# One product of a scaled V moved from VectorE to GpSimd in a fused attention and maxout kernel

## The chip, the cores and the metric

The kernel runs on one core of one Trainium2 chip. The metric is the device time of one execution in microseconds. A core has five engines that run their own instruction queues in order and meet at semaphores: TensorE (PE in the profile, with its weight loads as PEld), VectorE (DVE), ScalarE (ACT), GpSimd (POOL) and SyncE (SP), which here only issues DMAs.

## The reference

Four batches of eight heads over 768 positions of 64 dims are attended, causally in all heads, and in "streaming" heads only to 4 sink positions and a window of 64. Its output, laid out as 3072 tokens by 512, goes through a maxout layer with three weights of 512 x 768 and an output weight of 768 x 512.

```python
scores = scale * np.matmul(q, k.transpose(0, 1, 3, 2))
...
stream_keep = causal & (is_sink | in_win)
...
a = np.exp(scores)
a = a / (np.sum(a, axis=-1, keepdims=True) + 1e-09)
return np.matmul(a, v).astype(np.float32)
...
h = np.maximum(np.maximum(x @ w1, x @ w2), x @ w3)
return (h @ w_out).astype(np.float32)
```

## The kernel before, in words

The attention is cut into 16 steps. Step t belongs to batch t // 4, to half (t // 2) % 2 of the query positions, and to four heads (t % 2), which form two pairs i = 0 and 1. A batch's halves have 384 positions each, three blocks of 128. So step 2 is batch 0, second half, heads 0 to 3; step 3 the same with heads 4 to 7; step 4 begins batch 1.

A step goes through these functions:

- `scores(t, u)`: for each unit u of a step (two in a first half, four in a second) TensorE forms transposed scores in PSUM (L441) out of the tile KQ, ScalarE takes their exponentials into the fp16 tile pt (L452), and `masks` multiplies parts of pt by the head's mask in place (L479). This product is done by GpSimd, but for eight triples of step, pair and unit in the list `MASK_ON_DVE`, which VectorE does; (3, 0, 0), (3, 0, 1) and (3, 1, 3) are among them. The PSUM tiles of the scores come from a pool of two buffers.
- `prep_v(t, i, op, vf_engine)`: makes the fp16 values of a pair. First `op` casts the loaded fp32 values vs into va (L392). Then `vf_engine` multiplies them by the flags `far` of the heads into vf (L394), which is used for key blocks two or more behind the query block. In a second half vf is made from va for three blocks, 128 x 384 elements; so it waits for the cast.
- `av(t, i)`: TensorE multiplies pt by va and vf into one PSUM bank (L495; 30 matmuls in a second half), and VectorE takes the reciprocals of the sums (L503) and scales into x (L505).
- x is turned into xT either by a DMA transpose on SP's queue (L514, all steps in `BY_DMA`, step 2 among them) or by TensorE and a copy (`turn_x`; step 3).
- `ffn(b, half)`: a generator that yields after each group of matmuls. A group of four matmuls makes 128 x 384 of one of the three products (L338). The first weight's result is copied to acc by ScalarE (L346), the second and third are joined with it by VectorE's maximum (L349, into acc, and then hT). For batch 0 all groups of the first weight come first, then the second, then the third: six groups each. After them each of three blocks is multiplied by the output weight woutt (L364), copied to ot by ScalarE (L370) and written out by SP's queue (L371). The queue `fill(n)` emits n pieces of this work at a time.

The PSUM banks of `av`, of the transposes and of `ffn` come in turn from one pool of four, so a group of matmuls may have to wait until the result of four groups before has been read.

For batch 0, k and q are cast and transposed on TensorE (`cast_pair`, `turn_pair`). For later batches `load` brings k and q in by GpSimd's DMA queue (L174) and `turn` transposes them in blocks on VectorE into KQ (L190), two instructions for k and two for q of each four heads. The values of batches 1 to 3 are loaded on SP's queue by `load_v`; those of the second half of batch 0 by GpSimd's queue.

The order of all this is written by hand. Steps 0 and 1 stand in straight code; from step 2 on the table `PROGRAM` has one row for each unit of scores. A row has a number of `ffn` pieces that are due, a flag on whether the two pairs' scores are apart, and four strings of other work: ahead of the scores, behind them, and after each part of the filling. In the strings, `v 2 0 ad` is `prep_v` for step 2 and pair 0, with its cast on ScalarE (a) and its product on VectorE (d); `ap` puts the product on GpSimd. `cast`, `pair`, `load`, `load_v`, `turn`, `av` and `x` are the functions above; `gate` makes SP's queue wait for an exponential of step 3 before it loads the next values.

The rows around the change, with the units that they belong to, are those of units 2 and 3 of step 2 and units 0 to 2 of step 3:

```python
(2.0, False, "", "pair 1 2", "load 1 1", ""),
(2.2, False, "pair 1 3", "v 2 0 ad", "", "v 2 1 ap"),
(2.2, False, "", "gate, load_v 1 0", "", ""),
(1.6, True, "", "av 2 0", "", "turn 1 0 0 0"),
(1.0, True, "turn 1 0 0 1", "", "av 2 1, turn 1 0 1 0", ""),
```

In the second of them VectorE copies a transposed pair (L162), scores of unit 3 are formed, pair 0's values are prepared, some pieces of `ffn` are emitted, and pair 1's values are prepared. Each engine's queue takes its own instructions in this order: VectorE has that copy, the product of pair 0, and then the maxima of the `ffn` pieces; GpSimd has two masks of unit 3 and then the product of pair 1.

Of the kernel before, what the change touches and what calls it, by code (L numbers as in the profile page):

```python
# [51 lines left out]
def kernel(  # L52
# [94 lines left out]
    def turn_pair(half, hp, *engines):  # L147
        if (0, hp // 2) not in KQs:
            KQs[0, hp // 2] = qkt.tile([P, 2, S, 2], FP16, tag="KQ", name="KQ")
        xs = cast.pop((half, hp))  # L150
        n = 2 // len(engines)
        for part, op in enumerate(engines):
            tr = bank([P, 1024], FP16, "tr")
            for i in range(n):
                for j in range(HB):
                    c = i * HALF + j * P
                    nc.tensor.transpose(
                        tr[:, c : c + P],
                        xs[part + i][:, j].rearrange("p h d -> p (h d)"),
                        ident,  # L160
                    )
            op(  # L162
                out=of_pair(hp)[
                    :, part : part + n, half * HALF : (half + 1) * HALF
                ].rearrange("p i (t j) -> p i t j", j=HB),
                in_=tr[:, 0 : n * HALF].rearrange("p (i j t) -> p i t j", i=n, j=HB),
            )
# [218 lines left out]
    def prep_v(t, i, op, vf_engine):  # L386
        b, half, qd = where(t)
        vs = staged_v[b, half]
        j, k0 = b % 2, half * HB
        hs = slice(4 * qd + 2 * i, 4 * qd + 2 * i + 2)  # L390
        vdst = va[j][:, hs, k0 : k0 + HB, 0:D]
        op(out=vdst, in_=vs[:, hs])  # L392
        k0, k1 = ((0, 1), (1, 4))[half]
        vf_engine.tensor_tensor(  # L394
            out=vf[j][:, hs, k0:k1, 0:D],
            in0=vs[:, hs, 0:1] if half == 0 else va[j][:, hs, k0:k1, 0:D],
            in1=far[:, hs, k0:k1].unsqueeze(3).to_broadcast([P, 2, k1 - k0, D]),
            op=ALU.mult,
        )
# [120 lines left out]
    def turn_x(t, i, op=None):  # L520
# [82 lines left out]
        (2.4, True, "", "", "cast 1 2 dp", ""),  # L603
        (2.4, False, "load 1 0", "", "cast 1 3 da", ""),
        (2.0, False, "", "pair 1 2", "load 1 1", ""),
        (2.2, False, "pair 1 3", "v 2 0 ad", "", "v 2 1 ap"),
        (2.2, False, "", "gate, load_v 1 0", "", ""),
        (1.6, True, "", "av 2 0", "", "turn 1 0 0 0"),
        (1.0, True, "turn 1 0 0 1", "", "av 2 1, turn 1 0 1 0", ""),
# [44 lines left out]
        v=lambda t, i, e: prep_v(int(t), int(i), ops[e[0]], engines[e[1]]),  # L654
# [6 lines left out]
        pair=lambda h, hp: turn_pair(int(h), int(hp), dve),  # L661
# [65 lines left out]
```

## Time and profile before

| what | us |
|---|---|
| median of four runs | 202.26 |
| lowest and highest of them | 201.56, 202.72 |
| the profiled execution, its own time | 202.22 |
| its span, first to last instruction | 200.3 |

| engine | busy us | share of the span |
|---|---|---|
| TensorE, matmuls | 189.4 | 95% |
| TensorE, weight loads | 109.3 | 55% |
| ScalarE | 131.6 | 66% |
| VectorE | 123.4 | 62% |
| GpSimd | 122.5 | 61% |

The granted TensorE clock is full speed (1.000) through the whole span. Of the 32 products into vf, 29 are on GpSimd and three on VectorE: two of 128 x 128 in the first half of batch 0 and the one of step 2's pair 0.

A row of the profile names the engine, the line of the kernel, the operation, the tile written and the tiles read (out<-in), the shape and type, and the count. In the timeline it is headed by the start in microseconds from the span's start and the length, and ends in brackets with how long the engine was idle before it and what ended that idle time. In the view of waits a row has who waited, for whom, the total in microseconds, how often, and the longest.

### The profile page before, as it was taken

What the parts mean: (1) busy time and instruction counts of PE and PEld (TensorE: products, weight loads), DVE (VectorE), ACT (ScalarE), POOL (GpSimd) and SP (SyncE); (2) the same over time, 40 slices, a digit from 0 to 9 for tenths busy, and PEclk for the clock granted to TensorE, in tenths of its full rate; (3) what the DMA queues carried; (4) which work ended last, traced back from release to release, by engine and by line L of the source; (5) the groups of instructions that cost most, each with busy time, mean ns of one, the idle gap of its engine ahead of it and who ended that gap; (6) DMA issues with size and microseconds to landing.
All of it is one profiled execution on the core that took longest, in us unless ns stands there. A gap on an engine that the chain in (4) does not pass through costs nothing.

```text
span 200.3 us, 5133 instructions
## 1 busy us (share of the span) xinstructions
PE 189.4 (95%) x2059; PEld 109.3 (55%) x2059; DVE 123.4 (62%) x242; ACT 131.6 (66%) x206; POOL 122.5 (61%) x153
## 2 busy tenths in 40 slices
PE   7897999796999999999999999999999999999992
PEld 2455554455566466574655465575555565755552
DVE  2798687999777838871554739961555234443540
ACT  4586798597875777666787685757768769313221
POOL 3599169579897915787969726699937547500000
PEclk9999999999999999999999999999999999999999
DMA  5999999997739993804359994502401250023004
GB/s 181 271 233 224 277 240 212 213 200 179 184 47 163 171 241 111 163 17 128 111 86 141 162 263 124 101 20 79 140 20 23 105 75 20 3 56 142 3 0 157
DMA packets 43245, 26.48 MB, mean 132 GB/s; under 512 B 33558, under 2 KB 38230, under 8 KB 43222
## 3 DMA queue, kind: packets, MB, share of 16 engines
q1 hardware_dynamic: 37206, 15.01, 35.0%
q0 software_dynamic: 4784, 10.23, 26.3%
q10 hardware_dynamic: 1232, 0.92, 1.5%
q8 instruction: 16, 0.26, 0.5%
q14 instruction: 7, 0.06, 0.1%
HBM read 25.17 MB, written 6.29 MB: 157 GB/s over the span
## 4 chain that ended last, share of the span: by engine, by line
PE 74%; DMA 10%; POOL 5%; DVE 3%; issue 2%; ACT 2%; SPq 1%; DVEq 0%; ACTq 0%; POOLq 0%
PE yy L338 39%; PE yy L364 13%; PE st L441 9%; PE oacc L495 9%; DMA vs<-in_v_dram 7%; PE yst L338 3%; DMA ks<-in_k_dram 2%; DVE KQ L190 2%; ACT pt L452 1%; DMA out_dram<-ot 1%; POOL vs L208 1%; POOL qs L126 1%; POOL ks L126 1%; PE yst L364 1%; ACT ot L370 1%
## 5 line engine op out<-in xcount | busy, mean ns | idle before, releaser
L479 POOL TENSOR_TENSOR pt<-pt,mk 128x512 f16<-128x512 f16 (+1 forms) x76 | 80.5, 1083 | 36.8 <-ACT pt L452 36.8
L452 ACT ACTIVATE pt<-st 128x1024 f16<-128x1024 f32 (+3 forms) x99 | 83.1, 894 | 21.1 <-PE st L441 20.3
L349 DVE TENSOR_TENSOR acc<-yy,acc 128x384 f16<-128x384 f32 x45 | 25.1, 558 | 28.3 <-PE yy L338 18.6
L338 PE MATMUL yy<-xT,w2t 128*128 128x384 f16 x180 | 35.9, 327 | 1.7 <-DVE hT L349 1.7
L338 PE MATMUL yy<-xT,w1t 128*128 128x384 f16 x180 | 36.1, 327 | 0.1
L338 PE MATMUL yy<-xT,w0t 128*128 128x384 f16 x180 | 35.6, 326 | 0.4 <-DVE xT L531 0.4
L346 ACT CAST acc<-yy 128x384 f16<-128x384 f32 x45 | 21.0, 485 | 17.0 <-PE yy L338 10.6
L364 PE MATMUL yy<-woutt,hT 128*128 128x512 f16 (+1 forms) x138 | 32.0, 375 | 0.0
L441 PE MATMUL st<-KQ 32*128 32x384 f16 (+4 forms) x560 | 28.5, 279 | 0.6 <-DVE KQ L190 0.5
L349 DVE TENSOR_TENSOR hT<-yy,acc 128x384 f16<-128x384 f32 x45 | 24.9, 558 | 6.7 <-PE yy L338 4.3
L495 PEld LDWEIGHTS <-pt 128*128 128x128 f16 x672 | 23.9, 97 | 5.4 <-issue 2.2
L338 PEld LDWEIGHTS <-w2t 128*128 128x128 f16 x192 | 17.6, 98 | 15.1 <-issue 4.0
L190 DVE STREAM_TRANSPOSE KQ<-kq 128x384 f32<-128x384 f32 x24 | 25.7, 1129 | 0.0
L338 PEld LDWEIGHTS <-w0t 128*128 128x128 f16 x192 | 18.2, 98 | 12.9 <-issue 1.0
L495 PE MATMUL oacc<-va,pt 128*128 128x65 f16 x352 | 24.8, 193 | 0.3 <-ACT va L392 0.3
L338 PEld LDWEIGHTS <-w1t 128*128 128x128 f16 x192 | 17.2, 98 | 12.8 <-issue 1.3
L370 ACT COPY ot<-yy 128x512 f32<-128x512 f32 x22 | 12.9, 588 | 15.5 <-PE yy L364 9.2
L495 PE MATMUL oacc<-vf,pt 128*128 128x65 f16 x320 | 21.1, 193 | 0.9 <-POOL vf L394 0.9
L364 PEld LDWEIGHTS <-hT 128*128 128x128 f16 x150 | 13.9, 98 | 14.5 <-issue 0.3
L441 PEld LDWEIGHTS <-KQ 32*128 32x128 f16 (+1 forms) x560 | 12.1, 93 | 17.3 <-issue 11.8
L505 DVE TENSOR_TENSOR x<-oacc,rc 128x384 f16<-128x384 f32 x32 | 17.8, 557 | 1.3 <-DVE rc L503 0.2
L503 DVE RECIPROCAL rc<-oacc 128x6 f32<-128x6 f32 x32 | 6.1, 192 | 20.1 <-PE oacc L495 20.0
(71 smaller groups left out, 130.0 us busy)
## 6 DMA issues: line engine op xcount, KB each, us to landing
out_dram<-ot SPq DMA_DIRECT2D x23, 256.0 KB, 3.1
vs<-in_v_dram SPq DMA_DIRECT2D x21, 256.0 KB, 6.1
kq<-in_k_dram POOLq DMA_DIRECT2D x6, 384.0 KB, 5.5
kq<-in_q_dram POOLq DMA_DIRECT2D x6, 384.0 KB, 7.7
qs<-in_q_dram ACTq DMA_DIRECT2D x4, 192.0 KB, 4.1
ks<-in_k_dram SPq DMA_DIRECT2D x4, 192.0 KB, 3.7
w0t<-in_moe_w_dram POOLq DMA_DIRECT2D x1, 768.0 KB, 7.2
ks<-in_k_dram POOLq DMA_DIRECT2D x2, 384.0 KB, 6.9
```

Of the source, the lines that this page charges most:

```text
L190: nc.vector.transpose(out=dst.rearrange("c (p j) -> c j p", j=n)[:, j0:j1], in_=src.rearrange("c (j i) -> c j i", i=R),)
L338: nc.tensor.matmul(yy[:, 0:HALF], w_t[wi][:, ks, ni * P : (ni + 1) * P], xT[b, half][ks].rearrange("p a t -> p (a t)"), start=(ks == 0), s ...
L346: nc.scalar.copy(out=acc[ni], in_=yy[:, 0:HALF])
L349: nc.vector.tensor_tensor(out=dst, in0=yy[:, 0:HALF], in1=acc[ni], op=ALU.max)
L364: nc.tensor.matmul(yo[:, 0:n], hT[ns][:, tb * P : (tb + 1) * P], woutt[:, ns, c : c + n], start=(ns == 0), stop=(ns == NNB - 1),)
L370: op(out=ot[:, c : c + n], in_=yo[:, 0:n])
L441: nc.tensor.matmul(sts[g // m][:, g % m, c0 : c0 + n * P], KQ[rows, 0, ki * P : (ki + 1) * P], KQ[rows, 1, t0 : t0 + n * P], start=(c0 == ...
L452: nc.scalar.activation(out=pts[t, i][:, u, h0 : h0 + m, 0:w], in_=st[:, :, 0:w], func=AF.Exp, scale=sc,)
L479: engine.tensor_tensor(out=x, in0=x, in1=m, op=ALU.mult)
L495: nc.tensor.matmul(o[:, qi, hl, 0 : D + 1], pt[:, u, hl, c : c + P], vv[:, 2 * hp + hl, ki, 0 : D + 1], start=(idx == 0), stop=(idx == len ...
L503: nc.vector.reciprocal(out=rc, in_=o[:, :, :, D])
L505: nc.vector.tensor_tensor(out=x, in0=o[:, :, :, 0:D], in1=rc.unsqueeze(3).to_broadcast([P, HB, 2, D]), op=ALU.mult,)
```

## The change

One letter of the table: the product that makes vf for pair 0 of step 2 is issued on GpSimd in place of VectorE. The cast into va stays on ScalarE, and the place in the program's order stays as it is, so that GpSimd's queue has two masks, the product of pair 0 and the product of pair 1.

```diff
-        (2.2, False, "pair 1 3", "v 2 0 ad", "", "v 2 1 ap"),
+        (2.2, False, "pair 1 3", "v 2 0 ap", "", "v 2 1 ap"),
```

## The prediction

> **What bounds the kernel now.** I read the page first, then the waits of TensorE (PE) over the whole span, and then the timeline of each engine around the moved instruction. The page's rows of busy time and of slices:
>
> ```profile
> PE 189.4 (95%) x2059; PEld 109.3 (55%) x2059; DVE 123.4 (62%) x242; ACT 131.6 (66%) x206; POOL 122.5 (61%) x153
> PE   7897999796999999999999999999999999999992
> ```
>
> TensorE is busy for 95% of the span, so the kernel is bound by TensorE nearly everywhere: a microsecond counts only if it shortens TensorE's own row. The waits of TensorE from 50 us to the end are one line, and over 30 to 50 us they are four (the last two lines below are of the same stretch, for ScalarE and GpSimd):
>
> ```profile
> PE st L441 <- DVE KQ L190: 0.5, 1, 0.5
> ...
> PE yy L338 <- DVE hT L349: 1.7, 1, 1.7
> PE oacc L495 <- POOL vf L394: 0.9, 1, 0.9
> PE tr L527 <- DVE x L505: 0.7, 1, 0.7
> ...
> ACT pt L452 <- PE st L441: 4.1, 4, 1.8
> POOL pt L479 <- ACT pt L452: 4.0, 3, 2.4
> ```
>
> The reader is to see two things. TensorE's longest wait here is 1.7 us, for VectorE's hT; and after 51 us it waits for almost nothing, so whatever TensorE is early at 51 us it is early at the end. The timelines of VectorE (DVE), GpSimd (POOL), ScalarE and TensorE show where the 1.7 us comes from (start, length, engine, line, count, idle time before it and what ended it):
>
> ```profile
> 30.98 0.95 DVE L162 COPY KQ<-tr 128x768 f16<-128x768 f16 x1
> 33.03 2.67 DVE L394 TENSOR_TENSOR vf<-va,far 128x384 f16<-128x384 f16 x1 [1.10 <-ACT va L392]
> 35.63 1.47 DVE L349 TENSOR_TENSOR hT<-yy,acc 128x384 f16<-128x384 f32 x3
> ...
> 33.00 2.27 POOL L479 TENSOR_TENSOR pt<-pt,mk 128x512 f16<-128x512 f16 x2
> 35.23 1.16 POOL L394 TENSOR_TENSOR vf<-va,far 128x384 f16<-128x384 f16 x1
> 36.35 0.66 POOL L479 TENSOR_TENSOR pt<-pt,mk 128x256 f16<-128x256 f16 x1
> 39.42 0.67 POOL L479 TENSOR_TENSOR pt<-pt,mk 128x256 f16<-128x256 f16 x1 [2.41 <-ACT pt L452]
> ...
> 33.74 0.82 PE L338 MATMUL yy<-xT,w2t 128*128 128x384 f16 x4
> 36.23 0.81 PE L338 MATMUL yy<-xT,w2t 128*128 128x384 f16 x4 [1.66 <-DVE hT L349]
> 36.97 0.61 PE L441 MATMUL st<-KQ 64*128 64x384 f16 x8
> ...
> 37.40 1.02 ACT L452 ACTIVATE pt<-st 128x1024 f16<-128x1024 f32 x1 [1.83 <-PE st L441]
> ```
>
> The DVE row at 33.03 is the instruction that the change moves. VectorE idles 1.10 us until ScalarE has cast va, and then sits in this product until 35.70, while GpSimd runs two masks that end at 35.27. Behind it in VectorE's queue stand three hT maxima; the first is done at 36.17, its PSUM bank comes free, and only then does TensorE start its sixth group of w2 (36.23), 1.66 us after the last matmul it had issued (33.74 to 34.56).
>
> **The change, part by part.**
>
> *Removed from VectorE:* one instruction of 2.67 us and the 1.10 us of idling for va ahead of it: 3.77 us in which VectorE did nothing else. The hT maxima behind it can start when their groups are ready. Groups 2 to 4 of w2 run on TensorE from 31.14 to 33.26, 0.65 us each, so their maxima (0.54 us each, from the row of three) end at about 32.5, 33.2 and 33.8. The bank for group 6 is free at 32.5, and TensorE goes on at 34.4 (the pitch after 33.74 is 0.65) instead of 36.23.
>
> *Added to GpSimd:* one product 128x384 f16. The fifteen such products that GpSimd already makes (vf from va, line 394) take 822 to 1158 ns, with a median of 829, so 0.83 us; the 1158 is the one at 35.23, which met VectorE's product at its end. It stands where the second pair's product stands now: GpSimd reaches it at 35.23, va having been cast by 33.4, so it costs no wait for input, and ends at 35.23 + 0.83 = 36.06. No DMA is issued in this step, and the loads of kq at 31.87 and 32.46 are ahead of it in GpSimd's queue; nothing on SP's queue moves. Queued behind it: the second pair's product (to 36.9), the masks of step 3 (to 37.6, and then the one at 39.42). GpSimd idled 2.41 us ahead of 39.42 and 1.45 us more ahead of 41.54, each time for ScalarE's exponentials, so 0.83 us is covered here three times over as long as those exponentials don't come over 3 us earlier.
>
> *A rule against the move.* The row is 0.83 us on GpSimd. On VectorE the product itself is about 0.43 us: it ended at 35.70, 0.43 us after the masks let go at 35.27. The Trainium skill (GPSIMD Engine Reference, section "Elementwise — side-by-side cycle accounting") says just this, that GpSimd takes about twice as long as VectorE for a product of two inputs; by that rule alone the move is a loss of 0.4 us. But what stands in the queue is not 0.43 but 2.67 us plus the idling, so by the rows it is 0.83 us on an engine with spare time for 3.77 us on one that holds TensorE up. I take the rows.
>
> *A second rule, on who is held up.* The same skill (SBUF — State Buffer, section "Who interferes with whom") says that VectorE with two SBUF inputs and GpSimd reading SBUF share a port that one instruction holds to its end, and the other waits. The trace agrees in three places: DVE masks of 128x512 take 0.42 us at 27.37 and 75.40, with GpSimd free, but 0.58, 0.60 and 0.99 us at 44.62, 52.34 and 55.77, each ending about 0.28 us after the GpSimd mask beside it. It does not fit the moved row: VectorE entered at 33.03, 0.03 us behind the first of two GpSimd masks, and should by the rule have had the port at 34.2, but waited through both. This matters for the two DVE masks of step 3 (128x256, 0.28 us each), which now meet a run of GpSimd work without a gap from 33.0 to about 38.2. By the rule the first (ready at 34.6) enters at 35.27 and ends at 35.4; by the moved row's example a mask can be held for two instructions, to 36.1. Either way hT 5 and 6 (0.54 us each) end by 37.3, before their matmuls at L364 come to them (about 37.9). Let in at 35.27, it makes the new product 0.05 to 0.2 us late, so I put that product's end at 36.06 to 36.25.
>
> *The new path on TensorE.* Group 6 runs 34.4 to 35.05; the scores of step 3's next unit follow, the second pair at 35.6 because the exponential that frees its bank ends at 35.57 (ACT row at 33.63, x2, 1.94 us). So TensorE reaches av 2 0 at about 35.8, and now waits for GpSimd's product: 0.25 to 0.45 us until 36.1 to 36.3. The 30 matmuls then take 0.95 us (37.51 to 38.46 in the trace before), and the first L364 group starts at 37.05 to 37.25, where it started at 38.46. Gain 1.2 to 1.4 us: 1.66 removed, less about 0.35 of new wait.
>
> *Does it last to 51 us?* woutt lands at 20.0 + 15.8 = 35.8, before 37.1. The four loads of kq land at 37.7, 39.5, 41.5 and 43.6 (issue plus landing time); the first transposes that read each start at 39.37, 42.24, 45.12 and 46.99, so the least slack is 1.7 us, just more than the gain. v of the next batch lands at 46.5 and its first cast stood at 49.87. The xT of step 2 goes by SP's DMA transposes, the last landing by 48.1, and is first read at 51.12. Exponentials, masks and copies of the following slots all start from TensorE, and shift with it. VectorE is nearly full from 39.37 to 50.5 (eight transposes of 1.0 us pitch, four reciprocals with their x, and masks); it starts that run when x of av 2 0 is made, which is 1.2 to 1.4 us earlier. So I let the whole gain through.
>
> *Sum.* On the profiled execution (202.22 us, span 200.3, so 1.9 us around it): -1.66 + 0.35 = -1.3, giving 200.9; this execution lies 0.04 us under the median of the runs shown, 202.26, so 200.95. The likeliest case alone spans 200.7 to 201.2.
>
> **The rivals.**
>
> *Held maxima, gain partly lost.* If the second DVE mask of step 3 (ready at about 36.5) is held for three GpSimd instructions, to 38.2, then x of av 2 0 ends at 39.1 instead of 39.45, the transposes start 0.35 us earlier, not 1.3, and of that VectorE's 0.31 us of idling at 44.31 gives some back: a gain of 0.35 to 0.7, 201.5 to 201.9. For it: the moved row itself was held for two. Against it: the three other places, held for one.
>
> *VectorE starved, slower than before.* One mechanism: GpSimd's run from 33.0 has no gap, since the new product fills what VectorE used, and the FIRST DVE mask of step 3 gets no port until the run ends at 38.2. Then hT 5 and 6 end at 39.3, the second mask at 39.55, x at 40.25 (39.45 before, so 0.8 late); two transposes (2.0), reciprocal and x (0.8) and two more (2.1) end at 45.15, where they ended at 44.31; 0.31 us of the lag falls into the idling there, and 0.35 to 0.5 stays: 202.6 to 202.75. If the mask that VectorE then reaches at 45.15 is held in the same way, behind GpSimd's cast and first product of step 3 (0.70 and 0.83 us at 44.86 and 45.65), up to 1.0 comes on top, 203.75. It decides from the point where that mask is held beyond about 37.6, which takes four GpSimd instructions in a row; the longest hold in this trace is two.
>
> *GpSimd becomes the last.* 0.83 us later from 36 us on, would reach TensorE through the product it waited for at 46.52 (0.9 us). Against it: the 3.85 us of GpSimd's idle time between. I count it with the first rival: gain 0.5, 201.8.
>
> **How the numbers follow.** The likeliest case has 0.67, the two partial losses together 0.18, starvation 0.15. About 0.5% of the time, 1.0 us, is what a measurement of this kernel can tell from no change. The likeliest case passes it in nearly all of its range (0.64 with what measurement blurs), the partial losses end within it, and about half of starvation goes over it with the second mask's price: faster 0.64, same 0.28, slower 0.08. The range: from 200.4 (the whole 1.66 and no new wait is 200.6, and 0.2 for spread of the runs) up to 202.6, which takes in the partial losses and the nearer end of starvation.
>
> **What the profile after would show.** TensorE's wait for VectorE's hT of 1.7 us gone, and in its place a wait of 0.2 to 0.5 us of oacc for GpSimd's vf near 36; L364 first at 37.0 to 37.3; sixteen GpSimd products vf from va and none on VectorE; the first kq transpose at 37.9 to 38.1; TensorE without waits from about 49.8. The forecast is wrong if a DVE mask of step 3 lasts over 1.5 us, if the first kq transpose waits for its DMA, or if TensorE's waits for x and KQ at 49 to 51 us grow by what was saved at 35.

## The result, and the profile after

The changed kernel takes 201.03 us (median of 30 runs, 200.31 to 202.3) against 202.13 us (49 runs of the kernel before in the same sessions): a ratio of 0.9952, with a 95% interval of 0.9941 to 0.9964, so 0.7 to 1.2 us faster. The profiled execution took 201.29 us with a span of 199.3 us. Forecast were 200.95 us and a range of 200.4 to 202.6.

The page's rows of busy time and of slices, of the kernel after:

```profile
PE 189.6 (95%) x2059; PEld 109.3 (55%) x2059; DVE 122.8 (62%) x241; ACT 131.7 (66%) x206; POOL 123.1 (62%) x154
PE   7897999996999999999999999999999999999992
```

VectorE has one instruction less and 0.6 us less busy time, GpSimd one more and 0.6 us more. That VectorE loses so little, though the row that left it was 2.67 us long, is explained by a mask that grew (below). TensorE's share is the same; what went is idle time. The waits over 30 to 50 us, of the kernel after (who waited, for whom, total us, times, longest):

```profile
ACT pt L452 <- PE st L441: 2.4, 4, 1.3
POOL pt L479 <- ACT pt L452: 2.0, 2, 1.8
...
PE st L441 <- DVE KQ L190: 0.8, 2, 0.5
PE oacc L495 <- POOL vf L394: 0.7, 1, 0.7
PE tr L527 <- DVE x L505: 0.6, 1, 0.6
```

The wait of 1.7 us for hT is gone. The one for KQ has grown from one instance to two. The timelines of TensorE, VectorE and GpSimd in the kernel after:

```profile
33.98 1.48 PE L338 MATMUL yy<-xT,w2t 128*128 128x384 f16 x8
35.39 0.87 PE L441 MATMUL st<-KQ 64*128 64x384 f16 x8
36.19 0.35 PE L495 MATMUL oacc<-vf,pt 128*128 128x65 f16 x2
37.26 1.46 PE L364 MATMUL yy<-woutt,hT 128*128 128x512 f16 x6
...
44.01 0.63 PE L441 MATMUL st<-KQ 32*128 32x384 f16 x16 [0.28 <-DVE KQ L190]
...
32.24 1.86 DVE L349 TENSOR_TENSOR hT<-yy,acc 128x384 f16<-128x384 f32 x3
34.93 2.31 DVE L479 TENSOR_TENSOR pt<-pt,mk 128x256 f16<-128x256 f16 x1 [0.83 <-ACT pt L452]
37.16 1.01 DVE L349 TENSOR_TENSOR hT<-yy,acc 128x384 f16<-128x384 f32 x2
38.09 0.56 DVE L479 TENSOR_TENSOR pt<-pt,mk 128x256 f16<-128x256 f16 x1
...
39.26 2.08 DVE L190 STREAM_TRANSPOSE KQ<-kq 128x384 f32<-128x384 f32 x2
...
33.23 2.29 POOL L479 TENSOR_TENSOR pt<-pt,mk 128x512 f16<-128x512 f16 x2
35.46 1.62 POOL L394 TENSOR_TENSOR vf<-va,far 128x384 f16<-128x384 f16 x2
37.03 1.47 POOL L479 TENSOR_TENSOR pt<-pt,mk 128x256 f16<-128x256 f16 x2
```

The rows of the kernel before that go with the mask at 34.93, the transposes at 39.26 and the first L364 are:

```profile
37.02 0.28 DVE L479 TENSOR_TENSOR pt<-pt,mk 128x256 f16<-128x256 f16 x1
...
39.37 2.08 DVE L190 STREAM_TRANSPOSE KQ<-kq 128x384 f32<-128x384 f32 x2
...
38.46 1.46 PE L364 MATMUL yy<-woutt,hT 128*128 128x512 f16 x6
```

The fifth and sixth group of w2 now follow each other (x8 at 33.98), and hT 2 to 4 are finished by 34.10. But the row to look at is the DVE mask at 34.93: 128x256, 0.28 us in the trace before, now 2.31 us. It stands there while GpSimd runs the end of its masks and both products, and behind it wait hT 5 and 6.

**Times counted from the first w2 matmul.** Where this matmul lies differs from execution to execution (29.2 to 31.9 us in the traces of this study; 29.27 and 31.87 in two of one and the same kernel). So the traces are compared from that matmul: to the first matmul of L364, and to the first w0 matmul of the next piece of `ffn`, after which TensorE waits for almost nothing. Both are differences of starts in the timelines. From that w0 matmul to the end of the span it is 149.2 us in every trace but one (149.4 with the first mask on GpSimd), so what is gained there is gained at the end. Three kernels were traced twice, and each pair agrees within 0.03 us at both points.

| kernel | first w2, us | to L364 | to w0 | gain at w0 | ratio to before, 95% interval |
|---|---|---|---|---|---|
| before | 29.63 | 8.83 | 21.49 | | |
| after | 29.87 | 7.39 | 20.23 | 1.26 | 0.9952, 0.9941 to 0.9964 |
| GpSimd idle beside the product | 30.12 | 7.27 | 19.95 | 1.54 | 0.9946, 0.9926 to 0.9965 |
| product behind hT (second run) | 29.27 | 7.27 | 19.93 | 1.56 | 0.9929, 0.9903 to 0.9954 |
| after, first mask on GpSimd | 29.31 | 7.39 | 20.06 | 1.43 | 0.9957, 0.9941 to 0.9973 |
| after, both masks on GpSimd | 30.12 | 7.39 | 20.10 | 1.39 | 0.9945, 0.9929 to 0.9960 |
| split, block 1 on VectorE | 29.71 | 7.27 | 20.39 | 1.10 | 0.9984, 0.9955 to 1.0012 |
| split, block 3 on VectorE | 29.49 | 11.04 | 24.05 | -2.56 | 1.0115, 1.0080 to 1.0150 |
| after, product made twice | 29.45 | 8.36 | 21.02 | 0.47 | 0.9993, 0.9976 to 1.0010 |
| kq load issued later | 30.00 | 7.27 | 19.93 | 1.56 | 0.9939, 0.9917 to 0.9961 |

Counted so, the change brings 1.44 us at L364 and 1.26 us at w0. The medians, in which the head varies, show 1.1. The granted clock of TensorE is 1.000 in both profiles, before and after. In the second split it is not, as told there.

### The profile page after: what moved, and what is told of

Its sections match the earlier page's. It is cut to its first block, busy times and chain, and to the rows that moved or that the text cites. A ratio compares the mean times of both kernels' runs of the same rounds, so it can differ in the third digit from the quotient of the medians.

```text
span 199.3 us, 5133 instructions
## 1 busy us (share of the span) xinstructions
PE 189.6 (95%) x2059; PEld 109.3 (55%) x2059; DVE 122.8 (62%) x241; ACT 131.7 (66%) x206; POOL 123.1 (62%) x154
## 4 chain that ended last, share of the span: by engine, by line
PE 78%; DVE 8%; DMA 4%; ACT 4%; issue 2%; POOL 2%; SPq 1%; ACTq 0%; POOLq 0%; DVEq 0%
PE yy L338 43%; PE yy L364 12%; PE st L441 10%; PE oacc L495 8%; DVE KQ L190 4%; PE yst L338 3%; ACT pt L452 3%; DMA ks<-in_k_dram 3%; DVE x L505 2%; DMA out_dram<-ot 1%; PE tr L157 1%; PE yst L364 1%; POOL kn L139 1%; DVE hT L349 1%; POOL qn L139 0%
## 5 line engine op out<-in xcount | busy, mean ns | idle before, releaser
L338 PE MATMUL yy<-xT,w1t 128*128 128x384 f16 x180 | 36.1, 327 | 0.1
L364 PE MATMUL yy<-woutt,hT 128*128 128x512 f16 (+1 forms) x138 | 32.0, 375 | 0.0
L364 PEld LDWEIGHTS <-hT 128*128 128x128 f16 x150 | 14.0, 98 | 14.6 <-DVE hT L349 0.4
```

The lines of the kernel that those rows point to most:

```text
L338: nc.tensor.matmul(yy[:, 0:HALF], w_t[wi][:, ks, ni * P : (ni + 1) * P], xT[b, half][ks].rearrange("p a t -> p (a t)"), start=(ks == 0), s ...
L364: nc.tensor.matmul(yo[:, 0:n], hT[ns][:, tb * P : (tb + 1) * P], woutt[:, ns, c : c + n], start=(ns == 0), stop=(ns == NNB - 1),)
```

## The experiments

Theory A: the product itself is short; VectorE was held in it by GpSimd's instructions, and what cost time were the three hT maxima behind it, whose PSUM bank TensorE needed. Against it stand B (the product is slow on VectorE by itself) and C (the amount of VectorE's work is what counts), and, on the missing part of the gain and on these readings, D (the landing of k sets VectorE's pace, not the hold), E (GpSimd becomes the last), F (the first result was luck of the start) and G (GpSimd's idle time makes the product free).

**GpSimd made idle beside the product.**

```diff
-    MASK_ON_DVE = ((2, 0, 1), (3, 0, 0), (3, 0, 1), (3, 1, 3), (5, 0, 0), (5, 1, 0), (5, 1, 1), (7, 0, 1))
+    MASK_ON_DVE = ((2, 0, 1), (2, 0, 3), (2, 1, 3), (3, 0, 0), (3, 0, 1), (3, 1, 3), (5, 0, 0), (5, 1, 0), (5, 1, 1), (7, 0, 1))
```

> The kernel before, with the product left on VectorE, but the two GpSimd masks that ran beside it (step 2, unit 3) put on VectorE as well, so GpSimd is idle when the product starts. VectorE has more work than before (two masks of 0.42 us). Theory A (the product is 0.43 us and was held for 2.2 us by GpSimd's masks): the product takes 0.4 to 0.5 us, hT 2 is done by about 34.1, TensorE's wait of 1.7 us for hT is gone, L364 starts at 36.8 to 37.1 instead of 38.5; ratio to before 0.992 to 0.994. Rival B (this product is slow on VectorE by itself, by its strides or its broadcast input): it takes 2.7 us again and hT is later than before by up to 0.5 us; ratio 1.000 to 1.003. Rival C (only the amount of VectorE's work counts): 0.8 us more work, ratio 1.000 to 1.004.

Its VectorE timeline:

```profile
32.42 0.43 DVE L479 TENSOR_TENSOR pt<-pt,mk 128x512 f16<-128x512 f16 x1
33.12 0.42 DVE L479 TENSOR_TENSOR pt<-pt,mk 128x512 f16<-128x512 f16 x1 [0.28 <-ACT pt L452]
33.52 0.56 DVE L394 TENSOR_TENSOR vf<-va,far 128x384 f16<-128x384 f16 x1
```

The same product takes 0.56 us on VectorE when no GpSimd mask runs beside it, against 2.67. With more work than before, VectorE is in time, TensorE's wait for hT is gone, and 1.54 us are gained at w0. B and C fall. 0.56 is a little over the 0.43 that I had read off the end of the held row. Against GpSimd's 0.83 us the ratio is 1.5, where the Trainium skill (GPSIMD Engine Reference, "Elementwise — side-by-side cycle accounting") has 1.96 for an addition of 2048 fp32 elements; the direction agrees.

**The product behind the hT maxima, still on VectorE**, run twice.

```diff
-        (2.2, False, "pair 1 3", "v 2 0 ad", "", "v 2 1 ap"),
+        (2.2, False, "pair 1 3", "", "", "v 2 0 ad, v 2 1 ap"),
```

> The kernel before, with the product left on VectorE, but issued behind the three hT maxima of its row instead of ahead of them; the work of every engine is the same. Theory A (what cost 1.7 us is that three maxima stood behind a held instruction): hT 2 to 4 end by 34.1, TensorE does not wait for hT, and waits for the product at av 2 0 instead, until 35.8 to 36.6, according to how many GpSimd instructions hold it; L364 at 36.8 to 37.5; ratio 0.992 to 0.996. Rival C (the engine's load is what counts, so the move to GpSimd was needed): no gain, 0.999 to 1.001.

> The same kernel as in the run with the product left on VectorE behind the three hT maxima, timed again, because its few undisturbed runs leave the ratio wide (0.9884 to 0.9928) and it may be the fastest version. Theory A: from the first matmul of w2 to the first of L364 7.27 us as in its first trace (8.83 before, 7.39 after), 1.55 us gained to the end; ratio 0.991 to 0.9935, and below that of the kernel after. Rival F (the first run's ratio was luck of the start, whose length varies by some tenths of a microsecond from run to run): ratio 0.995 as after.

The first time gave a median of 200.38 us and a ratio of 0.9906 (0.9884 to 0.9928), on six runs, the second 200.56 us and 0.9929, on 13. The profiled execution of the first took 202.92 us, with the first w2 matmul at 31.87, so its head was over 2 us longer; from that matmul on, both traces have 7.27 us to L364. VectorE and GpSimd in the second:

```profile
31.65 1.86 DVE L349 TENSOR_TENSOR hT<-yy,acc 128x384 f16<-128x384 f32 x3
33.42 1.93 DVE L394 TENSOR_TENSOR vf<-va,far 128x384 f16<-128x384 f16 x1
35.28 0.91 DVE L479 TENSOR_TENSOR pt<-pt,mk 128x256 f16<-128x256 f16 x1
...
32.65 2.28 POOL L479 TENSOR_TENSOR pt<-pt,mk 128x512 f16<-128x512 f16 x2
34.88 1.16 POOL L394 TENSOR_TENSOR vf<-va,far 128x384 f16<-128x384 f16 x1
```

The product is held for as good as two masks again, 1.93 us, and nothing is lost, because the maxima are ahead of it. No engine's work was changed. So moving it to the other engine wasn't needed to free TensorE: the place in VectorE's queue was enough, and by the trace this version is 0.3 us better than the change: vf is ready in time, and the first mask of step 3 takes 0.91 us in it and not 2.31. F falls: the trace repeats. The interval of the second run overlaps that of the change, so by the times alone the 0.3 us is not settled.

**Work or hold: the product split.** First block 1 was left on VectorE, and blocks 2 and 3 went to GpSimd; then block 3 was left there, and blocks 1 and 2 went to GpSimd.

```diff
+        if (t, i) == (2, 0):
+            parts = [(vf_engine, 1, 2), (nc.gpsimd, 2, 4)]
...
```

```diff
+        if (t, i) == (2, 0):
+            parts = [(nc.gpsimd, 1, 3), (vf_engine, 3, 4)]
...
```

The dots stand for the loop that issues the same product once for each of the parts.

> The kernel before, with two thirds of the product (blocks 2 and 3) on GpSimd behind its masks and one third (block 1, 128x128) left on VectorE in its old place. Theory A (held work costs the hold, whatever its size): the third lasts 2.3 to 2.5 us on VectorE, TensorE waits 1.4 to 1.6 us for hT as before; ratio 0.998 to 1.001. Rival C (what counts is how much work VectorE has): two thirds of what the whole move brought, 0.9965 to 0.9975.

The first split missed its expectation: the row of VectorE's third is 0.28 us long at 31.93, ahead of the cast and of GpSimd's masks. Blocks 1 and 2 come from the first half's cast, so this third had nothing to wait for, which I had overlooked. TensorE's wait for hT is gone; this product shows nothing on the size of held work. The first mask of step 3 was held here as well, for 2.09 us through three GpSimd instructions (34.77 to 36.87), and 1.10 us are gained at w0. The ratio of 0.9984 doesn't contradict that: in eight of the 14 runs the granted clock was 0.989 to 0.991, and they took 202.06 to 203.45 us; the six at 0.996 or more, the profiled one among them, took 200.37 to 201.53. What lowered the clock in the eight, no trace shows.

> The kernel before, with blocks 1 and 2 of the product on GpSimd behind its masks and only block 3 (128x128) on VectorE in the old place. Block 3 is the one that is made from the cast of this step (blocks 1 and 2 come from the first half's cast, which is why the third left on VectorE in the first split ran at once, in 0.28 us). Theory A (held work costs wait and hold, whatever its size): VectorE waits 1.1 us for the cast, the third lasts 2.3 to 2.5 us instead of 0.28, held through two masks, TensorE waits 1.4 to 1.6 us for hT; from the first w2 matmul to the first w0 matmul of the next piece 21.2 to 21.6 us (21.49 before, 20.23 after); ratio 0.998 to 1.001. Rival C (what counts is how much work VectorE has): two thirds of the gain, 20.6 us, ratio 0.9965.

Block 3 is the one that needs the new cast. VectorE, GpSimd and TensorE in the second split:

```profile
32.89 3.75 DVE L394 TENSOR_TENSOR vf<-va,far 128x128 f16<-128x128 f16 x1 [1.10 <-ACT va L388]
36.56 1.48 DVE L349 TENSOR_TENSOR hT<-yy,acc 128x384 f16<-128x384 f32 x3
...
32.86 2.27 POOL L479 TENSOR_TENSOR pt<-pt,mk 128x512 f16<-128x512 f16 x2
35.09 1.39 POOL L394 TENSOR_TENSOR vf<-va,far 128x256 f16<-128x256 f16 x2
36.44 0.72 POOL L479 TENSOR_TENSOR pt<-pt,mk 128x256 f16<-128x256 f16 x1
...
37.16 0.83 PE L338 MATMUL yy<-xT,w2t 128*128 128x384 f16 x4 [2.74 <-DVE hT L349]
37.92 1.03 PE L441 MATMUL st<-KQ 64*128 64x384 f16 x8
...
40.53 1.81 PE L364 MATMUL yy<-woutt,hT 128*128 128x512 f16 x6
```

A product of a third of the size, 0.28 us when free, takes 3.75 us: it got in only when both masks and both products of GpSimd were over (36.48). C, which expected a gain of two thirds, falls for good: VectorE has less to do, and TensorE's sixth group of w2 starts 1.08 us later than before (2.74 us of idling ahead of it against 1.66).

That is not the whole of the 2.56 us lost at w0. The page's row of the granted clock, in slices of 5 us, is

```profile
PEclk9999999799999999999999999999999999999998
```

Behind the 2.74 us of idling the granted clock of TensorE was 0.50 from 38 to 41 us, and it was 1.00 again from 41.5. In that stretch the scores took 1.03 us (0.61 before), av 2 0 1.65 (0.95), and the six matmuls of L364 1.81 (1.46). The other 1.5 us were lost there. In the kernel before TensorE idled 1.66 us at this place, and the clock stayed at 1.00. Five of the six runs of this split had a mean clock of 0.989 to 0.992 and took 204.74 to 204.94 us; the sixth, at 1.000, took 203.19, which is 0.5% more than the 202.24 of the kernel before in the same session. So the longer hold alone costs 1.08 us against the kernel before, and the 1.15% contain a lower clock. That the longer idling brought it about fits the order of events, but no run tested it.

My expectation of 2.3 to 2.5 us for the product was wrong: the run of GpSimd that holds was lengthened by the two blocks put there, and the hold with it.

**How much of GpSimd's run holds.** In the kernel before, the loads of kq are issued behind the masks of unit 3.

```diff
-        (2.0, False, "", "pair 1 2", "load 1 1", ""),
-        (2.2, False, "pair 1 3", "v 2 0 ad", "", "v 2 1 ap"),
+        (2.0, False, "", "pair 1 2", "", ""),
+        (2.2, False, "pair 1 3", "v 2 0 ad, load 1 1", "", "v 2 1 ap"),
```

> The kernel before, product on VectorE in its old place, but GpSimd issues the loads of kq 1 1 behind its two masks of step 2's unit 3 instead of ahead of them, so that only one of the two masks is still to run when VectorE starts the product. Theory A (the hold lasts as long as GpSimd's masks run on): the product takes about 1.6 us instead of 2.67, TensorE's wait for hT falls from 1.7 to about 0.7 us, L364 comes 1.0 to 1.3 us earlier, less if the kq loads, 2.2 us later, are then waited for at the third and fourth pair of transposes; ratio 0.994 to 0.997. Rival B (the product or its hold has a fixed length): 2.7 us again, ratio 1.000 to 1.004.

VectorE and GpSimd:

```profile
33.40 0.56 DVE L394 TENSOR_TENSOR vf<-va,far 128x384 f16<-128x384 f16 x1 [1.10 <-ACT va L392]
33.88 1.48 DVE L349 TENSOR_TENSOR hT<-yy,acc 128x384 f16<-128x384 f32 x3
35.27 0.80 DVE L479 TENSOR_TENSOR pt<-pt,mk 128x256 f16<-128x256 f16 x1
...
31.14 3.83 POOL L479 TENSOR_TENSOR pt<-pt,mk 128x512 f16<-128x512 f16 x3
33.46 1.52 POOL L479 TENSOR_TENSOR pt<-pt,mk 128x512 f16<-128x512 f16 x1
34.92 0.59 POOL L174 DMA_DIRECT2D kq<-in_k_dram  x1
```

The row of 1.52 us is the last of the three in the row above it. The effect was in the forecast direction and larger: the product starts 0.1 us before the end of a mask and gets in ahead of the next, which takes 1.52 us instead of 1.16. All 1.56 us are gained. Here the same instruction in the same place of VectorE's queue is not held at all, only because GpSimd's masks run 1.0 us earlier, counted from the first w2 matmul (2.35 us after it, 3.37 before). That one mask more would hold it, as I had expected under theory A, was wrong. The mask at 35.27 took 0.80 us beside nothing but two DMA issues of GpSimd; the first experiment's masks at 32.42 and 33.12, beside such issues too, took their usual 0.42. I can't say why.

**Where the forecast's gain was lost.** The two VectorE masks of step 3 were put on GpSimd in the kernel after, first one, then both.

```diff
-    MASK_ON_DVE = ((2, 0, 1), (3, 0, 0), (3, 0, 1), (3, 1, 3), (5, 0, 0), (5, 1, 0), (5, 1, 1), (7, 0, 1))
+    MASK_ON_DVE = ((2, 0, 1), (3, 0, 1), (3, 1, 3), (5, 0, 0), (5, 1, 0), (5, 1, 1), (7, 0, 1))
```

```diff
-    MASK_ON_DVE = ((2, 0, 1), (3, 0, 0), (3, 0, 1), (3, 1, 3), (5, 0, 0), (5, 1, 0), (5, 1, 1), (7, 0, 1))
+    MASK_ON_DVE = ((2, 0, 1), (3, 1, 3), (5, 0, 0), (5, 1, 0), (5, 1, 1), (7, 0, 1))
```

> The kernel after, with the first VectorE mask of step 3 (pair 0, unit 0) moved to GpSimd too. In the trace after it took 2.31 us, held through three GpSimd instructions, and delayed hT 5 and 6 and all behind them on VectorE. Theory A (that hold is where the missing 0.3 us of the forecast went): hT 5 and 6 end by about 36, but the second mask (unit 1) then meets the same GpSimd run, now one mask longer (to about 39.0), and may be held for one to three of its instructions; ratio to before 0.992 (held for one) to 0.996 (held to the end). Rival D (VectorE's stretch is set by the landing of k or by TensorE, not by the hold): same as after, 0.995.

> The kernel after, with both VectorE masks of step 3 (pair 0, units 0 and 1) moved to GpSimd. Theory A: no VectorE instruction with two SBUF inputs is left beside GpSimd's run from 33 to 39.7; hT 5 and 6 end by 36, x of av 2 0 by 38.1, the first kq transpose starts at 37.9 to 38.1 (after 39.3), the wait of 0.28 us for KQ at 44 is gone, and the whole 1.3 to 1.5 us is gained: ratio to before 0.9925 to 0.9935. Rival D: no change against after, 0.995. Rival E (GpSimd becomes the last): its run lengthens by 1.3 us, the masks of step 3's unit 2 or the product that TensorE waits for at 45.5 come later, and the ratio is 0.997 or more.

With one mask moved, VectorE's other mask takes 0.98 us, kq's first transpose starts 8.6 us after the first w2 matmul instead of 9.4, the wait for KQ at 44 is gone, and w0 comes 0.17 us earlier than in the kernel after. That closes the sum: of the 0.3 us by which the change stays behind the reordered kernel, 0.12 are lost ahead of L364, where TensorE waits for the product (7.39 against 7.27), and 0.17 behind it, through the held mask. With both moved, the row that limits in the trace is another:

```profile
37.71 0.20 DVE L503 RECIPROCAL rc<-oacc 128x6 f32<-128x6 f32 x1 [1.41 <-PE oacc L495]
37.94 0.56 DVE L505 TENSOR_TENSOR x<-oacc,rc 128x384 f16<-128x384 f32 x1
39.37 2.08 DVE L190 STREAM_TRANSPOSE KQ<-kq 128x384 f32<-128x384 f32 x2 [0.88 <-DMA kq<-in_k_dram]
```

VectorE is ready 0.88 us before k has landed, so in this execution D holds too. But k landed late in it, 9.2 us after the first w2 matmul (9.0 in the first experiment), and 6.1 to 8.4 us after it in the other traces, that of the version with one mask moved among them (7.9). With the 8.0 us of the trace before, VectorE would not have waited here. That the transfer limits this version is thus shown for one execution alone. The two versions recover 0.17 and 0.13 us at w0, too little for the times to tell (0.9957 and 0.9945, both intervals around the 0.9952 of the change), and the expected 0.9925 to 0.9935 did not come. E falls.

**The price on GpSimd.** In the kernel after, the moved product is made twice.

```diff
-        vf_engine.tensor_tensor(
+        for _ in range(2 if (t, i) == (2, 0) else 1):
+            vf_engine.tensor_tensor(
```

> The kernel after, with the moved product made twice on GpSimd, one behind the other, into the same place. It doubles the cost that the change puts on GpSimd. Theory A (GpSimd's product is now what TensorE waits for at av 2 0, so its length goes one to one into the time): 0.83 us more from the first w2 matmul to L364 (8.2 us), and 0.6 to 0.9 us more to the end than after; ratio to before 0.998 to 1.001. Rival G (GpSimd's 3.85 us of idle time covers it): as after, 0.995.

L364 starts 0.97 us later than in the kernel after, w0 0.79 us later, and the ratio is 0.9993: one more product of 0.83 us leaves no gain that the times can tell from none, and 0.47 us by the trace. G falls, and so does the thought that GpSimd's idle time makes its work free here: that idle time is behind av 2 0, and the product is ahead of it. TensorE's waits, 31 to 60 us:

```profile
PE oacc L495 <- POOL vf L394: 1.8, 2, 0.9
PE tr L527 <- DVE x L505: 0.7, 1, 0.7
PE st L441 <- DVE KQ L190: 0.5, 1, 0.5
```

**Is the hold chance?** The kernel after and the one with the product made twice, in which the hold differs, were profiled once more.

> The kernel after once more, for its profile alone. The first VectorE mask of step 3 was held through three GpSimd instructions in the first trace (2.31 us). If the hold is fixed by the order of the instructions, 2.3 us again, with TensorE's wait for KQ of 0.2 to 0.4 us at 44; if it is a matter of nanoseconds who gets in, 0.75 us (one instruction) in some executions, and then no wait for KQ.

> The kernel with the product made twice once more, for its profile alone. There the same mask was held through one instruction only (0.75 us), though GpSimd's timing up to that point is the same within 0.02 us; its second product waits for the end of the first. If the hold is fixed by what stands in GpSimd's queue behind the running instruction, 0.75 us again; if by nanoseconds, 2.3 us or more in some executions.

The first VectorE mask of step 3 in the kernel after, and then in the one with the product made twice:

```profile
34.30 2.31 DVE L479 TENSOR_TENSOR pt<-pt,mk 128x256 f16<-128x256 f16 x1 [0.83 <-ACT pt L452]
```

```profile
34.40 0.76 DVE L479 TENSOR_TENSOR pt<-pt,mk 128x256 f16<-128x256 f16 x1 [0.83 <-ACT pt L452]
```

2.31 us again, and 0.76 (0.75 in the first trace). In both kernels the length of the hold repeated in the second execution, as it did in the reordered kernel (1.94 and 1.93 us), so it goes with the program rather than with chance. In the kernel with the doubled product, GpSimd's second product has to wait for its first, and VectorE's mask gets in ahead of the first. This fits the thought that what stands ready in GpSimd's queue decides, but no run tested it, and the rule was not found.

## Why the prediction was right, and where it was not

- *What bounds the kernel, and the removal.* Right. The wait of 1.66 us went, group 6 starts at once, and what had stood in the way was the held instruction at the head of VectorE's queue, as the first two experiments show.
- *0.83 us on GpSimd, to 36.06 to 36.25.* Right: the two products take 1.62 us together, and the first ends 6.43 us after the first w2 matmul, which is 36.06 in the times of the trace before. No VectorE mask made it later. The product's own length on VectorE, read as 0.43 us, is 0.56.
- *The new wait on TensorE, 0.35 us.* Nearly right in the total, not in its parts. The gain at L364 is 1.44 us where 1.2 to 1.4 were forecast. By the starts, group 6 comes 1.83 us earlier (4.77 us after the first w2 matmul, 6.60 before), the scores behind it give back 0.27, mostly for their bank (0.87 us against 0.61), and the product 0.12 (7.39 against 7.27 us where vf is ready in time). The sum of the forecast, 1.66 less 0.35, sets an idle time beside a wait and hides these parts. The wait for vf was put at 0.25 to 0.45 and was too large, since TensorE comes to av 2 0 0.15 us later than I had it. The experiment with two products shows that this wait is real.
- *The hold of step 3's first mask.* Wrong. I let it be held for one or two instructions, "to 36.1"; it was three, to 37.08, and repeatably so. My sign for a failed forecast, a mask over 1.5 us, did occur.
- *"So I let the whole gain through."* This is the step that failed, by a small amount. hT 5 and 6, the second mask (0.56 us), and x came late. Counted from the first w2 matmul, the first kq transpose started 0.35 us earlier than before (9.39 against 9.74 us) and not 1.2 to 1.4, and TensorE came to the scores at 44.01 0.36 us late, with 0.28 us of idling for KQ in the row. Of that the later waits gave back 0.18 us (for vf 0.75 us instead of 0.90, for x 0.63 instead of 0.66). It is the forecast's first rival, with the first mask in place of the second and the same 0.35 us at the transposes. It was cheaper than priced because the lag shrank on the way: the third transpose came 0.61 us earlier than before and the fifth 1.23, and TensorE had 0.54 us in hand at KQ before (made by 44.31, used at 44.85).
- *The two misses cancelled*, which is luck: 0.14 us more at L364 than the middle of the forecast, 0.18 less behind it, so 1.26 us stands against 1.3.
- *Starvation, slower than before.* It did not happen to the changed kernel. The second split shows that such a hold exists, through four instructions in a row. It made TensorE's sixth group 1.08 us later than before; the other 1.5 us of its loss came with the lower clock, for which the forecast had no term.
- *The slack of the kq loads, 1.7 us, "just more than the gain".* Not reached in the kernel after. It is no fixed number: in the two executions in which k landed late, 1.0 us or more behind the 8.0 us of the trace before, VectorE waited 0.78 and 0.88 us for it.

## What to carry to other kernels

When an elementwise instruction of VectorE is far longer than its kin, look at what GpSimd runs beside it before you blame its shape, and then at what stands behind it in its own queue: reordering the queue was worth at least as much here as moving the work. When a variant loses more than the waits explain, as the second split did, look at the granted clock before you blame the wait alone. An instruction with two SBUF inputs is dangerous at the head of a queue next to a long unbroken run of GpSimd products, however small it is; making that run longer, as this change does, moves the hold to the next such instruction. And an engine's idle time pays for added work only if it lies ahead of the point where the result is needed.

## What the runs showed of the hardware that was not expected

VectorE's instructions with two SBUF inputs were held through one GpSimd instruction (0.75 us), two (2.67 and 1.93), three (2.31 and 2.09) and four (3.75), although each waits from its start on. The Trainium skill (SBUF — State Buffer, "Summary: rules for kernel authors") has the second to issue blocked until the first finishes; that describes the cases of one, and not the others, in which GpSimd's later instructions went ahead of a VectorE instruction that had been waiting. Maxima with one input in PSUM (0.54 to 0.56 us beside GpSimd's masks) were not held in the traces read here. In the other direction, a GpSimd mask that met VectorE's product took 1.52 us instead of 1.16. And in the second split the granted clock fell to 0.50 for about 3 us behind 2.74 us of TensorE's idling, while it stayed at 1.00 behind the 1.66 us of the kernel before.
